# Differences of sequence blocks in a spectral layer: formed at their use instead of stored

## The chip, the cores and the metric

The kernel runs on one core of a Trainium2 chip. The metric is the device time of one execution in microseconds (us); less is better. The engines named here are PE (matrix products), DVE (element-wise work on vectors), ACT (copies and casts), POOL (element-wise work too, idle in the stages of this text) and SP, whose queue issues the DMA transfers.

## The reference

Four residual layers work on x, a sequence of S = 2048 rows of D = 640 numbers in float32: attention, spectral, attention, spectral. The attention layers (sliding, dilated, 32 heads) aren't touched by the change. The spectral layer, on the layer-normed x, is

```
a = x @ hid_re.T        # hidden DFT, real part
b = x @ hid_im.T        # hidden DFT, imaginary part
y = seq_re @ a - seq_im @ b
x = x + y
```

with the 2048 x 2048 DFT matrices seq_re, seq_im and the 640 x 640 matrices hid_re, hid_im as inputs. The result must agree with float32 arithmetic.

## The kernel before

The layers are li = 0 to 3; spectral ones are li = 1 and li = 3 (class LayerB). Each first multiplies the sequence matrices with x, writes the products z to DRAM, and then applies the hidden matrices in the stage called hidden here (`hid_mm`, L1393, with its operands prepared on ACT and DVE at L1365 to L1384).

Products are float32 in effect: an operand is split into a high half (ACT's cast, L1137) and a low half (DVE's subtraction, L1138), and a block product is three matmul passes over the halves. A split writes one of a ring of split buffers: 8 in li = 1, 10 in li = 3 (`views`).

The sequence product of six of the eight tiles of 256 columns is done by `pair(p)` for p = 0, 1, 2. One pair multiplies two such tiles t1, t2 by a block scheme with seven products instead of eight, in two sweeps of 8 steps each:

- The first sweep loads the blocks b11, b21, b22, b12 per step (128 x 512 numbers, 256 KB each) straight from the DFT matrix in DRAM (`s_raw`, L1126, DRAM name cs_in), splits all four, and runs 30 matmuls per step (L1148). In li = 1 it also forms t1 = b12 - b11 and t3 = b22 - b12 on DVE (L1225) and stores both in a DRAM tile tb (L1227). In li = 3 it doesn't.
- The second sweep needs x1 = b12 - b11, x3 = b22 - b12, x2 = b22 - x1 and x4 = b21 - x2. It loads x1 and x3 back from tb (L1221) and b22 and b21 from the DFT matrix, forms x2 and x4 on DVE (L1225), splits all four and runs 24 matmuls per step, in the order x2 (banks aux), x3 (t), x4 (m), x1 (xt and pq). Both spectral layers have the same DFT matrix, so li = 3 reads what li = 1 has stored.

A loaded block goes to one of nine raw buffers: five with the tag win, two xa and two slices of one tile e. A difference is formed in place, in the buffer of one of its operands. A raw buffer is free for the next load when the low half of its block has been split off; the load then goes out on SP's queue.

After the second sweep the banks are drained by ACT (L1301) and DVE (L1303 to L1313). In the last pair (p = 2) of a layer the hidden stage's operands are loaded meanwhile, and DVE starts preparing them (L1366, L1378, L1379, L1382) among the last steps. In li = 1 the first sweeps also carry the preparation of the hidden matrices (`b_prep`, L1177 to L1191).

The program is built ahead of the run: a scheduler with a cost model sets the order of the instructions on each engine, and picks among the free buffers of a tag. Inside `pair` only PE's order is written by hand (`manual_schedule`); in the hidden stage PE's and SP's are. DVE, ACT and the queue then run their lists in that order, each instruction waiting for what it needs.

## Time and profile before

| | us |
|---|---|
| median of 3 runs (1698.45 to 1706.01) | 1699.35 |
| span of the profiled execution | 1700.9 |
| its own time beside the span | not shown |
| PE busy | 1679.7 (99%) |
| DVE busy | 1339.2 (79%) |
| ACT busy | 794.0 (47%) |
| pairs of li = 1 | 438 to 735 |
| pairs of li = 3 | 1275 to 1574 |

How to read the rows below: a row of the timeline has the start, the duration, the engine, the line of the kernel, the operation, the tile written and the tiles read, their shape, a count, and in brackets the idle time before it with what released it. Tile names are those of the buffers: aux, t, m, xt and pq are banks of PE's output; win, xa and e are raw buffers; zo, e, stg, ot and pr are split buffers (e names both kinds); cs_in is the DFT matrix. A row of the stretches has begin and end, then the length, and for PE, PEld (weight load), DVE, ACT and POOL the busy time with the count, then PE's granted clock (1.00 is full), the DMA share and GB/s. A row of DMA issues ends with the size and the median from issue to landing.

### The profile page before, as it was taken

What the parts mean: (1) busy time and instruction counts of PE and PEld (TensorE: products, weight loads), DVE (VectorE), ACT (ScalarE), POOL (GpSimd) and SP (SyncE); (2) the same over time, 40 slices, a digit from 0 to 9 for tenths busy, and PEclk for the clock granted to TensorE, in tenths of its full rate; (3) what the DMA queues carried; (4) which work ended last, traced back from release to release, by engine and by line L of the source; (5) the groups of instructions that cost most, each with busy time, mean ns of one, the idle gap of its engine ahead of it and who ended that gap; (6) DMA issues with size and microseconds to landing.
All of it is one profiled execution on the core that took longest, in us unless ns stands there. A gap on an engine that the chain in (4) does not pass through costs nothing.

```text
span 1700.9 us, 25512 instructions
## 1 busy us (share of the span) xinstructions
PE 1679.7 (99%) x8558; PEld 1464.6 (86%) x8558; DVE 1339.2 (79%) x2034; ACT 794.0 (47%) x1617; POOL 625.8 (37%) x588
## 2 busy tenths in 40 slices
PE   9999999989999999999999999999999999999999
PEld 7888988868888887899988889988888888888999
DVE  6999999978588786788639999999784656657784
ACT  5664644544354443536554335444444544444231
POOL 4899999950000000000028988999400000000000
PEclk9999999999999999999999999999999999999999
DMA  8996668857899989986377866788666776787942
GB/s 295 315 322 227 221 227 307 271 206 265 287 370 322 370 270 354 351 331 225 122 226 239 270 217 204 246 284 295 212 234 208 225 228 215 242 282 270 362 164 93
DMA packets 263139, 441.13 MB, mean 259 GB/s; under 512 B 21824, under 2 KB 126016, under 8 KB 260704
## 3 DMA queue, kind: packets, MB, share of 16 engines
q1 hardware_dynamic: 259808, 437.55, 75.7%
q10 hardware_dynamic: 3200, 1.97, 0.4%
q8 instruction: 67, 1.10, 0.3%
q14 instruction: 64, 0.52, 0.1%
HBM read 319.75 MB, written 119.67 MB: 258 GB/s over the span
## 4 chain that ended last, share of the span: by engine, by line
PE 76%; DVE 10%; POOL 6%; DMA 4%; issue 2%; ACT 0%; SPq 0%; DVEq 0%; POOLq 0%; ACTq 0%
PE m L381 19%; PE t L1148 7%; PE aux L1148 7%; PE m L1148 7%; PE pq L1148 5%; PE xt L1148 5%; PE m L1393 4%; PE aux L1393 4%; PE m L1004 3%; PE t L1004 3%; DVE pr L450 2%; PE aux L531 2%; DVE pr L490 2%; POOL pr L509 2%; PE xt L1393 2%
## 5 line engine op out<-in xcount | busy, mean ns | idle before, releaser
L381 PE MATMUL m<-r,s 128*128 128x480 f32 x1920 | 434.5, 381 | 0.6 <-ACT stg L388 0.4
L381 PEld LDWEIGHTS m<-r,s 128*128 128x128 f32 x1920 | 355.4, 188 | 53.5 <-ACT stg L388 0.8
L193 POOL TENSOR_TENSOR stats<-stats,mhalf 128x1 f32<-128x1 f32 (+1 forms) x40 | 29.2, 730 | 512.2 <-ACT stats L189 503.8
L509 POOL TENSOR_TENSOR pr<-pr 128x640 f32<-128x640 f32 x126 | 207.8, 1650 | 23.1 <-DVE pr L490 21.7
L450 DVE TENSOR_TENSOR pr<-pq,win 128x1280 f32<-128x1280 f32 x128 | 189.9, 1484 | 13.8 <-DMA win<-kvb 7.8
L490 DVE TENSOR_TENSOR pr<-pq,win 128x1280 f32<-128x1280 f32 x128 | 190.3, 1487 | 3.7 <-POOL zo L511 1.2
L453 POOL TENSOR_TENSOR pr<-pr 128x640 f32<-128x640 f32 x115 | 164.9, 1434 | 11.2 <-DVE pr L450 11.2
L460 DVE TENSOR_REDUCE lg<-pr 128x64 f32<-128x640 f32 (+1 forms) x128 | 112.7, 881 | 8.0 <-POOL pr L453 7.9
L510 POOL TENSOR_TENSOR pr<-pr 128x320 f32<-128x320 f32 x126 | 112.0, 889 | 9.9
L388 ACT COPY stg<-m 128x480 f32<-128x480 f32 x128 | 71.0, 555 | 92.9 <-PE m L381 69.1
L1004 PE MATMUL m<-s,r 128*128 128x512 f32 x366 | 111.2, 392 | 1.6 <-DMA s<-c0b 1.3
L1004 PE MATMUL t<-s,r 128*128 128x512 f32 x366 | 110.3, 390 | 0.0
L531 PE MATMUL aux<-r2a,ot 128*128 128x320 f32 x540 | 84.7, 310 | 0.7 <-ACT s L369 0.7
L531 PEld LDWEIGHTS aux<-r2a,ot 128*128 128x128 f32 x540 | 81.1, 188 | 2.8 <-ACT s L369 1.2
L1004 PEld LDWEIGHTS m<-s,r 128*128 128x128 f32 x366 | 67.6, 188 | 16.1 <-DMA s<-c0b 1.9
L1004 PEld LDWEIGHTS t<-s,r 128*128 128x128 f32 x366 | 68.7, 188 | 14.5
L1137 ACT CAST zo<-win 128x512 fp32r<-128x512 f32 x76 | 47.2, 621 | 65.4 <-PE xt L1148 30.0
L423 ACT COPY pq<-qs 128x320 f32<-128x320 f32 x64 | 27.5, 430 | 106.0 <-DVE pr L490 73.4
L1138 DVE TENSOR_TENSOR zo<-win,zo 128x512 fp32r<-128x512 f32 x76 | 52.1, 688 | 23.7 <-ACT zo L1137 23.3
L511 POOL TENSOR_TENSOR zo<-pr 128x160 f32<-128x160 f32 x126 | 67.1, 532 | 9.9
L1004 PE MATMUL xt<-s,r 128*128 128x512 f32 x183 | 68.6, 389 | 0.0
L468 ACT ACTIVATE lg<-lg 128x128 f32<-128x128 f32 x64 | 20.3, 317 | 74.6 <-DVE lg L479 74.4
(531 smaller groups left out, 3650.2 us busy)
## 6 DMA issues: line engine op xcount, KB each, us to landing
win<-cs_in SPq DMA_DIRECT2D x192, 256.0 KB, 3.8
win<-kvb SPq DMA_DIRECT2D x96, 440.0 KB, 5.3
win<-kvb SPq DMA_DIRECT2D x64, 360.0 KB, 5.0
kvb<-stg SPq DMA_DIRECT2D x60, 320.0 KB, 4.9
xa<-cs_in SPq DMA_DIRECT2D x66, 256.0 KB, 3.6
e<-cs_in SPq DMA_DIRECT2D x64, 256.0 KB, 3.9
r<-zb SPq DMA_DIRECT2D x12, 1280.0 KB, 5.9
win<-tb SPq DMA_DIRECT2D x56, 256.0 KB, 4.4
```

The lines of the kernel that those rows point to most:

```text
L381: nc.tensor.matmul(mt[g][:, : 3 * F], st[:, a, k], wq[q][:, b, k], start=n == 0, stop=n == 14)
L388: nc.scalar.copy(sgs[q][:, :, j % 2], mt.pop(g)[:, : 3 * F].rearrange("p (a f) -> p a f", f=FE))
L450: nc.vector.tensor_tensor(pr, q, wview(u, jp, 0, [[1, FE]]), op=ALU.mult)
L453: nc.gpsimd.tensor_tensor(pv[:, :, 0:10], pv[:, :, 0:10], pv[:, :, 10:20], op=ALU.add)
L460: nc.vector.tensor_reduce(lgs[u][:, :, 2 * jp : 2 * jp + 2].rearrange("p h j w -> p (j w) h"), prq.pop((u, jp)), axis=AX.X, op=ALU.add,)
L490: nc.vector.tensor_tensor(pr.rearrange("p j w (h d) -> p j w h d", d=DH), lgs[u][:, :, 2 * jp : 2 * jp + 2].rearrange("p h j w -> p j w h" ...
L509: g.tensor_tensor(pr[:, :, 0:4], pr[:, :, 0:4], pr[:, :, 4:8], op=ALU.add)
L510: g.tensor_tensor(pr[:, :, 0:2], pr[:, :, 0:2], pr[:, :, 2:4], op=ALU.add)
L531: nc.tensor.matmul(m[:, :320], oT[(c, j)][:, a, k], wo_s["w"][:, b, k, e * 320 : (e + 1) * 320], start=(i, k) == (0, 0), stop=(i, k) == (2 ...
L1004: self.last = nc.tensor.matmul(self.z[t][k], self.xn[c][:, a, j, k * P : (k + 1) * P], self.ct[s][:, b], start=s == 0 and i == 0, stop=s = ...
L1148: nc.tensor.matmul(bank, w(a, kb), hl[b], start=start and (a, b) == (0, 0), stop=stop and (a, b) == (1, 0), skip_group_check=True,)
L1393: nc.tensor.matmul(bank[:, :320], s[:, a, k], w[:, b], start=start and (k, a, b) == (0, 0, 0), stop=stop and (k, a, b) == (KD - 1, 1, 0), ...
```

## The change

The DRAM tile tb goes, with its stores in li = 1 and its reloads in both layers. First sweeps form no differences. Second sweeps load b11, b12, b22 and b21 from the DFT matrix and form x1, x3, x2, x4 from them on DVE, in that order in the code. Products and results stay as they were.

```diff
--- before.py
+++ after.py
@@ -130,7 +130,6 @@
     qb = [[dr.tile([P, 2, NJ, FE], F32, name=f"qb_{c}_{q}") for q in range(NQ)] for c in range(NC)]
     xcb = [{m: dr.tile([P, NP, 2, 256], F32, name=f"xc_{l}_{m}") for m in (1, 2, 4)} for l in range(2)]
     zb = [[dr.tile([P, 4, KD, P], F32, name=f"zb_{l}_{t}") for t in range(NT)] for l in range(2)]
-    tb = [dr.tile([P, NP, 2, 512], F32, name=f"tb_{p}") for p in range(NPAIR)]
     wbd = dr.tile([P, NB * KD, 2, 320], F32, name="wbd")
     c0b = dr.tile([P, NST, 2, 512], F32, name="c0b")
     wob = dr.tile([P, 2, KD, D], F32, name="wob")
@@ -1205,26 +1204,14 @@
             views = [("zo0", 1), ("zo1", 1), ("e0", 1), ("stg", 2), ("zo2", 1), ("e1", 1), ("stg", 2), ("ot", 1)]
             if self.li == 3:
                 views += [("pr2", 1), ("pr3", 1)]
-            names = ("t1", "t3")
-
             def raw(t, s):
                 return self.s_raw(t, s, tags)
 
             def split(x):
                 return self.s_split(x, views)
 
-            def t_slot(n, i):
-                return tb[p][:, i, names.index(n)].rearrange("p (r t) -> p r t", r=2)
-
-            def t_raw(n, i):
-                x = self.s_buf(tags)
-                nc.sync.dma_start(x, t_slot(n, i))
-                return x
-
-            def t_sum(n, i, o, a, b):
+            def t_sum(o, a, b):
                 v.tensor_tensor(o, a, b, op=ALU.subtract)
-                if n in names:
-                    nc.sync.dma_start(t_slot(n, i), o)
                 return o
 
             def k1(i):
@@ -1264,9 +1251,6 @@
                     self.product(f2, self.x_plain(*k2(i), 512), p22, i == 0, False)
                     p12 = split(b12)
                     self.product(f2, self.x_plain(*k1(i), 512), p12, False, i == NP - 1)
-                    if sums:
-                        t_sum("t1", i, b11, b12, b11)
-                        t_sum("t3", i, b12, b22, b12)
                     self.flush()
                     if self.bprep and (p == 0 or i > 1):
                         next(self.bprep, None)
@@ -1286,12 +1270,14 @@
                 self.nx = 0
                 for i in range(NP):
                     ends = i == 0, i == NP - 1
-                    x1, b22, x3, b21 = t_raw("t1", i), raw(t2, NP + i), t_raw("t3", i), raw(t1, NP + i)
+                    b11, b12, b22, b21 = raw(t1, i), raw(t2, i), raw(t2, NP + i), raw(t1, NP + i)
+                    x1 = t_sum(b11, b12, b11)
                     s1, s2, s3 = (self.x_slot(m, i, XTAGS) if last and (m, i) in self.xlate else self.x_kept(m, i) for m in (1, 2, 3))
-                    x2 = t_sum("t2", i, b22, b22, x1)
+                    x3 = t_sum(b12, b22, b12)
+                    x2 = t_sum(b22, b22, x1)
                     self.product(q, s2, split(x2), False, i == NP - 1)
                     self.product(r, s3, split(x3), *ends)
-                    x4 = t_sum("t4", i, b21, b21, x2)
+                    x4 = t_sum(b21, b21, x2)
                     self.product(w, self.x_plain(*k2(i), 256), split(x4), *ends)
                     self.product(y, s1, split(x1), *ends)
                     self.flush()
```

Which instructions stand where on the engines, before and after, follows from the scheduler. Line numbers are smaller by 1 to 14 in the new kernel: the difference is L1225 before and L1214 after, the low half L1138 and L1137, the hidden product L1393 and L1379. The number behind a tile's name is that of the buffer's use.

The first place is DVE in the middle of a first sweep of li = 1 (its first pair). Before, one step with the two differences, and with a preparation of the hidden matrices behind them:

```order
L1138 TENSOR_TENSOR zo_756_4790<-win_4781,zo_756_4790 128x512
L1138 TENSOR_TENSOR stg_4749<-win_4726,stg_4749 128x512
L1138 TENSOR_TENSOR zo_757_4799<-win_4783,zo_757_4799 128x512
L1225 TENSOR_TENSOR win_4781<-win_4787,win_4781 128x512
L1138 TENSOR_TENSOR e_758_4808<-xa_4785,e_758_4808 128x512
L1138 TENSOR_TENSOR stg_4826<-win_4787,stg_4826 128x512
L1225 TENSOR_TENSOR win_4787<-xa_4785,win_4787 128x512
L147 SCALAR_TENSOR_TENSOR pr_751_4778<-pr_741_4716,pr_751_4778 128x2x320
```

After, at the same place:

```order
L1137 TENSOR_TENSOR zo_756_4779<-win_4770,zo_756_4779 128x512
L1137 TENSOR_TENSOR stg_4742<-win_4719,stg_4742 128x512
L1137 TENSOR_TENSOR zo_757_4788<-win_4772,zo_757_4788 128x512
L1137 TENSOR_TENSOR e_758_4797<-xa_4774,e_758_4797 128x512
L1137 TENSOR_TENSOR stg_4815<-win_4776,stg_4815 128x512
L146 SCALAR_TENSOR_TENSOR pr_751_4767<-pr_741_4709,pr_751_4767 128x2x320
```

The two L1225 rows are gone, and each raw buffer is free at its split.

The second place is DVE in li = 1's last second sweep. Before, the rows of one step: both differences, x2 and x4, then the four splits:

```order
L1225 TENSOR_TENSOR win_7110<-win_7110,xa_7108 128x512
L1225 TENSOR_TENSOR win_7113<-win_7113,win_7110 128x512
L1138 TENSOR_TENSOR zo_1142_7119<-win_7110,zo_1142_7119 128x512
L1138 TENSOR_TENSOR stg_7138<-win_7113,stg_7138 128x512
L1138 TENSOR_TENSOR e_1143_7128<-e_724_4650,e_1143_7128 128x512
L1138 TENSOR_TENSOR ot_7147<-xa_7108,ot_7147 128x512
```

After, eight rows from the same stretch; the differences of step 3 (x1 into xa_7047, x3 into win_7049, x2 into e_724, and the first of step 4, into xa_7097) stand between the splits of step 2:

```order
L1214 TENSOR_TENSOR xa_7047<-win_7049,xa_7047 128x512
L1137 TENSOR_TENSOR zo_1134_7009<-win_6998,zo_1134_7009 128x512
L1137 TENSOR_TENSOR zo_1135_7018<-e_724_4647,zo_1135_7018 128x512
L1214 TENSOR_TENSOR win_7049<-e_724_4647,win_7049 128x512
L1137 TENSOR_TENSOR e_1136_7028<-win_7000,e_1136_7028 128x512
L1214 TENSOR_TENSOR e_724_4647<-e_724_4647,xa_7047 128x512
L1137 TENSOR_TENSOR stg_7037<-win_6995,stg_7037 128x512
L1214 TENSOR_TENSOR xa_7097<-win_7099,xa_7097 128x512
```

A step has eight rows in place of six, and the first of them reads two loads into buffers that splits two steps earlier have freed.

The third place is PE at the end of li = 3's last second sweep. Before, the last step's products are complete before the hidden stage's first burst (L1393):

```order
L1148 MATMUL m_2363_15055<-zo_2433_15439,r_1_1904_12264 128x512 x3
L1148 MATMUL m_2364_15056<-zo_2433_15439,r_1_1904_12264 128x512 x3
L1148 MATMUL xt_15057<-zo_2434_15448,zo_2421_15363 128x512 x3
L1148 MATMUL pq_15058<-zo_2434_15448,zo_2421_15363 128x512 x3
L1393 MATMUL aux_2449_15507<-r2a_15109,r_2_2409_15307 128x320 x15
```

After:

```order
L1147 MATMUL m_2363_15036<-zo_2433_15436,r_1_1904_12213 128x512
L1379 MATMUL aux_2449_15504<-r2a_15092,r_2_2409_15298 128x320 x15
L1147 MATMUL m_2363_15036<-zo_2433_15436,r_1_1904_12213 128x512 x2
L1147 MATMUL m_2364_15037<-zo_2433_15436,r_1_1904_12213 128x512 x3
L1147 MATMUL xt_15038<-zo_2434_15445,zo_2421_15357 128x512 x3
L1147 MATMUL pq_15039<-zo_2434_15445,zo_2421_15357 128x512 x3
L1379 MATMUL aux_2450_15505<-r2a_15092,r_2_2409_15298 128x320 x15
```

One burst of the hidden stage, into the first aux bank, now stands ahead of the last eleven matmuls of the sweep. On SP's queue the 48 stores are gone and 96 reloads have become loads of cs_in; POOL's rows are the same.

## The prediction

> **What bounds the kernel now.** I read the page's busy shares first, then a table of stretches (one per sweep, cut where PE's step pattern changes), then PE's waits inside the spectral layers.
>
> ```profile
> span 1700.9 us, 25512 instructions
> PE 1679.7 (99%) x8558; PEld 1464.6 (86%) x8558; DVE 1339.2 (79%) x2034; ACT 794.0 (47%) x1617; POOL 625.8 (37%) x588
> 635.20:691.48 56.28, 54.95 (x241) 44.97 (x240) 35.13 (x56) 21.06 (x35) 0.00 (x0) 1.00 0.99 353
> 691.48:735.00 43.52, 43.52 (x193) 36.04 (x192) 37.92 (x58) 23.98 (x39) 0.00 (x0) 1.00 0.83 294
> ...
> 1525.70:1574.00 48.30, 48.30 (x214) 39.98 (x213) 36.63 (x56) 24.67 (x42) 0.00 (x0) 1.00 0.78 270
> PE t L1148 <- ACT zo L1137: 1.1, 1, 1.1
> PE t L1148 <- DVE zo L1138: 0.2, 1, 0.2
> PE pq L1148 <- DVE s L1311: 0.2, 1, 0.2
> PE xt L1148 <- DVE s L1311: 0.2, 1, 0.2
> ```
>
> PE is busy 1679.7 of 1700.9 us, so at most 21 us can be won in the whole program. The three stretches are li=1's last first sweep, li=1's last second sweep and li=3's last second sweep with a little of what stands ahead of it. Behind the stretch's length come busy time and count of PE, PEld, DVE, ACT and POOL, then granted clock, DMA share and GB/s. In the second sweeps PE is busy for the whole stretch at clock 1.00. The four wait rows are all that PE waited in li=1's three pairs (430 to 740 us); the same question for li=3's pairs (1275 to 1575 us) answers with no row. So the edited code runs at PE's pace, and a gain is limited to those waits.
>
> PE's pace and DVE's are two stretches of the timeline:
>
> ```profile
> 696.92 1.52 PE L1148 MATMUL aux<-zo,s 128*128 128x512 f32 x6
> 698.28 1.52 PE L1148 MATMUL t<-e,r 128*128 128x512 f32 x6
> ...
> 702.36 1.52 PE L1148 MATMUL aux<-zo,zo 128*128 128x512 f32 x6
> 697.04 0.68 DVE L1138 TENSOR_TENSOR zo<-e,zo 128x512 fp32r<-128x512 f32 x1
> 697.64 0.68 DVE L1138 TENSOR_TENSOR e<-win,e 128x512 fp32r<-128x512 f32 x1
> 698.25 0.68 DVE L1138 TENSOR_TENSOR stg<-win,stg 128x512 fp32r<-128x512 f32 x1
> 698.85 0.68 DVE L1225 TENSOR_TENSOR win<-win,xa 128x512 f32<-128x512 f32 x1
> ```
>
> A product's six matmuls take 698.28 − 696.92 = 1.36 us, and a second-sweep step, aux to aux, 702.36 − 696.92 = 5.44. DVE's 512-wide subtraction, whether split (L1138) or difference (L1225), starts 0.60 us behind the one before it: (698.85 − 697.04) / 3 = 0.603, although 0.68 is recorded.
>
> **The stores that go.** One store tile is written in li=1 only:
>
> ```profile
> L1227 SPq DMA_DIRECT2D tb<-win x27: 319/327/1104, 425.9 to 681.1; - x27
> DMA to landing us min/median/max: 2.0/4.6/6.2
> L1126 SPq DMA_DIRECT2D win<-cs_in x158: 327/333/1402, 420.3 to 1554.8; - x158
> DMA to landing us min/median/max: 2.5/3.9/7.6
> ```
>
> There are 3 pairs × 8 steps × 2 = 48 stores (27 from win buffers) of 256 KB, 4.2 MB in each li=1 first sweep, where the DMA share is 0.99. SP issues 48 fewer at 0.33 us. What can be won is what PE waits there: 1.1 + 0.2 on the splits, and at most 0.2 + 0.2 more on bank evacuations that DVE does. I take −1.3, bounds 0 and −1.7. The 96 reloads become 96 loads of the DFT matrix, of the same size and on the same queue. All transfers on the stored tile land in a median 4.6 us and all plain loads in 3.9. The count per step stays four, so I put this swap at 0.
>
> **DVE's differences.** In li=1 48 subtractions move from the first sweeps to the second ones (a first sweep loses 16 × 0.60 = 9.6 us of DVE work); in li=3 48 are new. A second-sweep step goes from six to eight of these ops, 8 × 0.603 = 4.82 us against PE's 5.44. By throughput they are hidden, with 0.62 a step to spare. In the last pair of each layer, hidden-DFT preparation shares DVE, and that cover is gone for two or three steps; there the lead that DVE has built up must carry it.
>
> **The new way that loads come round.** This is the term on which the forecast rests. A step needs four of nine raw buffers. Before, the first split of a step needed two loads (the stored difference and b22); now x2 = b22 − (b12 − b11) needs three, and the third is issued one split later. From the release of a buffer by a split to the difference that reads its refill, three round trips in li=3's middle pair and one in li=1's last show the size:
>
> ```profile
> 708.98 0.69 DVE L1138 TENSOR_TENSOR stg<-xa,stg 128x512 fp32r<-128x512 f32 x1 [0.85 <-ACT stg L1137]
> 709.70 0.33 SPq L1126 DMA_DIRECT2D xa<-cs_in  x1
> 714.46 0.69 DVE L1225 TENSOR_TENSOR xa<-xa,win 128x512 f32<-128x512 f32 x1 [1.03 <-DMA xa<-cs_in]
> 1437.56 0.69 DVE L1138 TENSOR_TENSOR ot<-xa,ot 128x512 fp32r<-128x512 f32 x1
> 1438.53 0.38 SPq L1126 DMA_DIRECT2D xa<-cs_in  x1
> 1442.75 0.69 DVE L1225 TENSOR_TENSOR xa<-xa,win 128x512 f32<-128x512 f32 x1 [1.80 <-DMA xa<-cs_in]
> 1445.77 0.68 DVE L1138 TENSOR_TENSOR stg<-win,stg 128x512 fp32r<-128x512 f32 x1
> 1446.48 0.33 SPq L1126 DMA_DIRECT2D win<-cs_in  x1
> 1449.55 0.69 DVE L1225 TENSOR_TENSOR win<-win,e 128x512 f32<-128x512 f32 x1 [0.94 <-DMA win<-cs_in]
> 1450.76 0.68 DVE L1138 TENSOR_TENSOR ot<-xa,ot 128x512 fp32r<-128x512 f32 x1
> 1451.47 0.33 SPq L1126 DMA_DIRECT2D xa<-cs_in  x1
> 1455.79 0.69 DVE L1225 TENSOR_TENSOR xa<-xa,win 128x512 f32<-128x512 f32 x1 [0.97 <-DMA xa<-cs_in]
> ```
>
> From the split's end to the difference's start: 714.46 − 709.67 = 4.8, 1442.75 − 1438.25 = 4.5, 1449.55 − 1446.45 = 3.1, 1455.79 − 1451.44 = 4.35. I call this d; the mean is 4.2. The lead that absorbs it is how far DVE's splits run ahead of PE, limited by the split buffers (8 in li=1, 10 in li=3):
>
> ```profile
> 625.21 0.69 DVE L1138 TENSOR_TENSOR ot<-e,ot 128x512 fp32r<-128x512 f32 x1 [0.67 <-ACT ot L1137]
> 633.84 0.84 PE L1148 MATMUL xt<-ot,r2a 128*128 128x512 f32 x3
> 1464.74 0.69 DVE L1138 TENSOR_TENSOR pr<-win,pr 128x512 fp32r<-128x512 f32 x1 [0.67 <-ACT pr L1137]
> 1476.08 1.30 PE L1148 MATMUL aux<-pr,r 128*128 128x512 f32 x5
> 720.02 0.82 DVE L1378 TENSOR_TENSOR e<-r 128x640 f32<-128x640 f32 x1
> ...
> 721.49 0.68 DVE L1138 TENSOR_TENSOR stg<-win,stg 128x512 fp32r<-128x512 f32 x1
> ```
>
> Split end to matmul is 633.84 − 625.90 = 7.9 us in li=1 and 1476.08 − 1465.43 = 10.65 in li=3. A 640-wide preparation op costs (721.49 − 720.02) / 2 = 0.735.
>
> Now the dependences, counted along DVE's new order (each buffer followed by name from the split that frees it to the difference that reads its next load). In li=1's last pair, from the split of x1 in step 0 to the split of x4 in step 7, the longest chain holds 36 ops of 512, 8 of 640 and five round trips: 36 × 0.603 + 8 × 0.735 + 5d = 27.6 + 5d. PE needs between those two products 6.75 steps, 36.7 us. PE stands still for 27.6 + 5d − 36.7 − 7.9 = 5d − 17.0: at d = 3.1 nothing, at 4.0 3.0, at 5.0 8.0. In li=3's last pair the chain holds 39 and 12 ops and four trips: 32.3 + 4d − 36.7 − 10.65 = 4d − 15.0, so 0, 1.0 and 5.0. The other four second sweeps stay inside their leads: the nearest to its limit, li=1's first, has 29 ops, one preparation of 640 and five trips, 18.2 + 5d against seven steps' 38.1 and the lead of 7.9, and stalls from d = 5.6 only.
>
> I take d = 4.0, a little under the mean, because only trips that DVE had to wait for could be read off; those that came in time are not among them. That gives 3.0 + 1.0 = +4.0. The ends are the least and the largest quoted, 3.1 (nothing) and 4.8 (7.0 + 4.2).
>
> [...]
>
> **PE's own order** is altered at one place, the end of li=3's last second sweep: the first hidden burst (15 matmuls into aux) now stands ahead of the last eleven matmuls of step 7. It needs the copy of the aux bank by ACT (L1301) 11 × 0.227 = 2.5 us sooner than before. If it must wait for that copy, the bounds are 0 and 1.1, the largest wait for ACT in the rows above. I take 0.2, because seven matmuls (1.6 us) still lie between aux's last product and the burst.
>
> **Sum.** −1.3 + 0 + 4.0 + 0.2 = +2.9 on the profiled execution's 1700.9 us. Its own time beside the span isn't shown; the span is 1.5 us above the median of 1699.35 us, so I add the difference to the median: 1702.2, said as 1702 us.
>
> **The rivals.**
> *Loads come round too slowly (slower).* With more traffic d is longer. The two last pairs also fetch the hidden layer's operands:
>
> ```profile
> win<-cs_in SPq DMA_DIRECT2D x6, 256.0 KB, 5.4
> win<-cs_in SPq DMA_DIRECT2D x13, 256.0 KB, 2.9
> ```
>
> The first row is li=1's last second sweep, where loads into this tile land in a median 5.4 us; the second is li=3's middle one, with 2.9. If all trips in both last pairs carry 1 us more (d = 5.0), the waits are 8.0 + 5.0 and the result +11.9, about 1711; with the full 2.5 us more that the rows differ by (d = 6.5) it is 15.5 + 11.0, about 1725. This becomes slower by over 0.5% from a stall of 9.8 us, where 9d − 32.0 = 9.8: d = 4.6. For it: the one trip quoted from that pair is the longest. Against it: that pair's trip had a landing inside its 4.8, so 5.4 is not the landing of every load, and before the change PE waits nowhere in these stretches.
>
> *DVE itself becomes the bound (slower).* If each op held DVE for the recorded 0.69, a step would need 5.52 against 5.44, and the chains would grow by 36 × 0.09 = 3.2 and 3.5 us; with d = 4.0 the stall is 6.2 + 4.5, the result +9.6, about 1709. The quoted starts 0.60 apart speak against it. [...]
>
> *Relief of the DMA queue (faster).* In li=1's first sweeps 4.2 MB of about 20 per sweep go (353 GB/s × 56.28 us). But PE waits only 1.7 there, so alone this gives 1697.6, not a measurable gain.
>
> *The cover holds (no change).* PE hides every difference and load: with the stores' relief 1698, without it 1699.
>
> **How the numbers follow.** This measurement can tell about 0.5%, 8.5 us, from no change: below 1690.9 and above 1707.8. My forecast (d between 3.1 and 4.6, with small stalls) has 0.45, and no stall with or without the 1.3 us gain 0.23: together 0.68 within 0.5%. Slow loads have 0.24, DVE's longer ops 0.03, the moved burst or something else in the new order that costs over 8 us 0.02: 0.29 slower. Faster has 0.03, since no row shows 8.5 us to win. The range runs from 1696 (all bounds on the good side, 1699.35 − 1.7, and the spread of the three runs shown) to 1714 (d = 5.2, 9.0 + 5.8 of stall); beyond it I leave the worse half of the slow loads.
>
> **What would show it.** PE's waits in li=1's first sweeps should be near zero, and DMA share there fall by a fifth. In the second sweeps DVE's busy time should rise to 8 ops a step. New waits of PE should name ACT or DVE splits of the spectral line and lie only in steps 3 to 7 of the last pairs, a few us together. Behind the end of li=3's last sweep aux should not wait. I am wrong if PE waits in first or middle pairs too, if DVE's starts spread past 0.60 without a wait, or if the time falls below 1691 us.

## The result, and the profile after

The changed kernel takes 1717.91 us (median of 4 runs, 1716.14 to 1718.88); the kernel before, run beside it, takes 1702.49 (4 runs, 1698.45 to 1706.01). The ratio is 1.009, with a 95% interval of 1.0068 to 1.0111: slower by 15 us. The forecast of no change was wrong, and the time lies above the range (1696 to 1714). The side was that of the first rival. Its cause was another one, as the experiments show.

The page of the changed kernel, its first rows:

```profile
span 1714.0 us, 25517 instructions
PE 1686.6 (98%) x8558; PEld 1467.3 (86%) x8558; DVE 1361.3 (79%) x2082; ACT 789.6 (46%) x1617; POOL 626.0 (37%) x588
```

The span has grown by 13.1 us. PE runs the same 8558 matmuls, and DVE has 48 instructions more. The waits of PE in li = 1's pairs (430 to 740 us) and then in li = 3's (1275 to 1600 us); the columns are total, number and longest:

```profile
PE aux L1147 <- ACT zo L1136: 2.5, 1, 2.5
PE aux L1147 <- DVE zo L1137: 2.4, 3, 1.3
PE aux L1147 <- ACT s L1259: 1.1, 1, 1.1
PE xt L1147 <- DVE s L1297: 0.9, 1, 0.9
PE m L1147 <- DVE s L1292: 0.6, 2, 0.4
PE pq L1147 <- DVE s L1297: 0.2, 1, 0.2
...
PE aux L1147 <- DVE pr L1137: 1.2, 1, 1.2
PE aux L1147 <- DMA zo<-xc: 0.2, 1, 0.2
```

Before there were 1.7 us of such waits in li = 1 and none in li = 3; now there are 7.7 and 1.4. They name splits (L1136 on ACT, L1137 on DVE), copies and sums of finished banks (L1259, L1292, L1297) and, in li = 3, one load. The table of stretches of the changed kernel, for the last pair's two sweeps (cut about 1 us ahead of the start of each):

```profile
639.00:692.80 53.80, 53.80 (x239) 44.55 (x239) 32.09 (x49) 21.08 (x35) 0.00 (x0) 1.00 0.87 294
692.80:745.00 52.20, 48.45 (x202) 39.34 (x201) 43.63 (x68) 23.54 (x41) 0.00 (x0) 0.93 0.74 256
```

The relief of the DMA queue is there: the last first sweep moves 294 GB/s where it moved 353. The last second sweep has become the worst stretch, with a wait of PE and a granted clock of 0.93 where it was 1.00.

To see where the time went, I compare the start of the second product (bank t) of each sweep in the two traces. In the first pair's second sweep, for instance, it starts at 494.22 before and 494.89 after, so PE is 0.7 us behind there. The table holds this lag, in us, against the profiled execution of the kernel before (positive is behind), for the experiments too (their names are those used below). "End of li=1" is the end of the last pair's last product; the last column is the difference of the spans:

| kernel | li=1 starts | last pair starts | its second sweep | end of li=1 | li=3's last second sweep | span |
|---|---|---|---|---|---|---|
| the change | −0.7 | 4.8 | 2.9 | 9.7 | 10.6 | 13.1 |
| before, again | −0.4 | −0.3 | −1.4 | −1.4 | −0.6 | −0.8 |
| only li=3 changed | −1.5 | 0.1 | −1.0 | −1.0 | −1.2 | 1.0 |
| only li=1's second sweeps | −2.4 | 0.6 | 6.3 | 13.0 | 11.4 | 11.5 |
| differences later | 0.4 | 9.7 | 7.8 | 13.1 | 13.1 | 20.3 |
| x1, x3 on POOL | −0.5 | 14.4 | 13.6 | 22.0 | 25.1 | 31.4 |
| no x1, x3 | −1.3 | 4.4 | 2.5 | 2.5 | 2.7 | 7.0 |
| before, two more ops | −0.1 | 0.9 | −0.6 | 0.3 | 0.3 | 5.4 |
| preparation of hidden operands later | −1.2 | 4.8 | 2.9 | 4.0 | 5.2 | 5.4 |
| preparation of hidden matrices later | 1.5 | 0.6 | −1.3 | 2.4 | 1.9 | 4.6 |
| both preparations later | 1.0 | 2.4 | 0.5 | 0.5 | 2.3 | 2.3 |
| all three later | −0.4 | 0.9 | −1.0 | −0.2 | −0.2 | −0.1 |

The 13.1 us of the change are thus: −0.7 ahead of the pairs, +5.5 in the first two pairs of li = 1, −1.9 in its last first sweep, +6.8 in its last second sweep, +0.9 between the layers, and +2.5 from li = 3's last second sweep on. Two executions of one kernel differ by up to 1.4 us in a column ("before, again"), so differences of that size carry nothing.

The largest piece is a single stall. The timeline of the changed kernel at the last step of li = 1, first PE, then DVE, then ACT:

```profile
735.08 0.80 PE L1147 MATMUL aux<-zo,pr 128*128 128x512 f32 x1 [2.48 <-ACT zo L1136]
737.16 2.50 PE L1147 MATMUL aux<-zo,pr 128*128 128x512 f32 x5 [1.28 <-DVE zo L1137]
739.45 2.68 PE L1147 MATMUL t<-e,r 128*128 128x512 f32 x6
741.97 1.55 PE L1147 MATMUL m<-stg,r 128*128 128x512 f32 x6
...
731.08 1.55 DVE L1352 TENSOR_TENSOR r<-r,r 128x640 fp32r<-128x640 f32 x2
...
733.27 0.69 DVE L1214 TENSOR_TENSOR xa<-xa,win 128x512 f32<-128x512 f32 x1
...
735.68 0.82 DVE L1352 TENSOR_TENSOR zo<-r,zo 128x640 fp32r<-128x640 f32 x1
736.42 0.69 DVE L1137 TENSOR_TENSOR zo<-xa,zo 128x512 fp32r<-128x512 f32 x1
...
733.79 0.72 ACT L1351 CAST zo<-r 128x640 fp32r<-128x640 f32 x1
734.42 0.61 ACT L1136 CAST zo<-xa 128x512 fp32r<-128x512 f32 x1
```

x2 of step 7 is formed at 733.27 into xa, cast at 734.42 and has its low half at 736.42. Ahead of it stand two preparation ops of 640 on DVE (L1352 at 731.08), one more ahead of its low half (735.68), and a preparation cast on ACT (L1351) ahead of its cast. PE, which needs x2 first of the four, waits 2.48 + 1.28 = 3.76 us. It loses more: from the first aux matmul to the second are 2.08 us in place of 0.23, the five behind it take 739.45 − 737.16 = 2.29 in place of 1.13, the six of t take 2.52 in place of 1.36. With the 2.48 that is 1.85 + 1.16 + 1.16 more, 6.7 us, the whole lag of that sweep. Its granted clock (third number from the end) in the 10 us around the wait and in the piece in which it is low:

```profile
730.00:740.00 10.00, 6.25 (x20) 4.42 (x19) 9.88 (x15) 5.15 (x9) 0.00 (x0) 0.75 0.34 135
735.07:741.90 6.83, 5.54 (x12) 4.11 (x13) 5.69 (x10) 3.63 (x6) 0.00 (x0) 0.50 0.16 33
```

So some 2.9 of the 6.7 us are a lower clock behind the wait, and 3.8 are the wait.

The second place is the first pair's second sweep, ACT, PE and DVE of the changed kernel:

```profile
492.14 0.74 ACT L144 ACTIVATE pr<-pr 128x640 fp32r<-128x640 f32 x1 [3.85 <-DMA wbd<-pr]
492.78 1.05 ACT L1259 COPY s<-aux 128x512 f32<-128x512 f32 x2
493.40 1.66 PE L1147 MATMUL aux<-zo,r2a 128*128 128x512 f32 x6 [1.10 <-ACT s L1259]
499.75 1.42 PE L1147 MATMUL aux<-zo,r2a 128*128 128x512 f32 x5 [0.39 <-DVE zo L1137]
...
497.68 0.69 DVE L1214 TENSOR_TENSOR win<-xa,win 128x512 f32<-128x512 f32 x1 [2.74 <-DMA xa<-cs_in]
499.01 0.69 DVE L1137 TENSOR_TENSOR zo<-win,zo 128x512 fp32r<-128x512 f32 x1
```

An op of the hidden matrices' preparation (`b_prep`, L144) holds ACT for 3.85 us, because the tile it writes is still being stored (wbd). The copy of bank aux stands behind it, and PE behind the copy. In step 1 DVE waits 2.74 us for a load, and the split of x2 (499.01) comes as late.

### The profile page after: what moved, and what is told of

It reads as the page before. It is cut to its first block, busy times and chain, and to the rows that moved or that the text cites. A ratio compares the mean times of both kernels' runs of the same rounds, so it can differ in the third digit from the quotient of the medians.

```text
span 1714.0 us, 25517 instructions
## 1 busy us (share of the span) xinstructions
PE 1686.6 (98%) x8558; PEld 1467.3 (86%) x8558; DVE 1361.3 (79%) x2082; ACT 789.6 (46%) x1617; POOL 626.0 (37%) x588
## 4 chain that ended last, share of the span: by engine, by line
PE 54%; DVE 19%; DMA 13%; POOL 8%; issue 4%; ACT 2%; SPq 1%; DVEq 0%; ACTq 0%; POOLq 0%
PE m L380 11%; PE aux L1147 5%; PE t L1147 5%; PE m L1147 5%; DVE pr L449 4%; PE aux L1379 4%; PE pq L1147 4%; PE xt L1147 4%; DVE pr L489 3%; PE m L1379 3%; POOL pr L508 3%; PE m L1003 2%; PE t L1003 2%; DMA e<-cs_in 2%; POOL pr L452 2%
## 5 line engine op out<-in xcount | busy, mean ns | idle before, releaser
L1136 ACT CAST zo<-win 128x512 fp32r<-128x512 f32 x76 | 47.1, 621 | 75.7 <-PE xt L1147 38.9
L1137 DVE TENSOR_TENSOR zo<-win,zo 128x512 fp32r<-128x512 f32 x76 | 52.0, 688 | 20.2 <-ACT zo L1136 19.9
L1147 PE MATMUL t<-e,r 128*128 128x512 f32 x204 | 53.0, 396 | 0.0
```

What stands on the lines that cost most here:

```text
L1147: nc.tensor.matmul(bank, w(a, kb), hl[b], start=start and (a, b) == (0, 0), stop=stop and (a, b) == (1, 0), skip_group_check=True,)
```

## The experiments

Each is compared with the kernel before, run on the same chip; ratios have 95% intervals. The first question was which layer loses.

**One layer at a time.** The store tile stays in both kernels; the named layer alone loads plain blocks.

```diff
+                    plain = self.li == 3      # the other kernel: == 1
+                    if plain:
+                        x1, x3, b22, b21 = raw(t1, i), raw(t2, i), raw(t2, NP + i), raw(t1, NP + i)
+                        v.tensor_tensor(x1, x3, x1, op=ALU.subtract)
+                    else:
+                        x1, b22, x3, b21 = t_raw("t1", i), raw(t2, NP + i), t_raw("t3", i), raw(t1, NP + i)
...
+                    if plain:
+                        v.tensor_tensor(x3, b22, x3, op=ALU.subtract)
```

> Only li=3 is changed: li=1 still stores its two differences and reloads them, li=3 loads plain blocks and forms all four differences on VectorE. Three theories. (H) DVE takes its list in order, so a difference that waits for a load holds up splits that are ready behind it, and the lead over PE is used up; what tips it over in li=1 is the work that rides along there (b_prep in the first pairs, hidden preparation in the last). (D) DVE has too many instructions where other work rides along. (L) it is the load's round trip alone, in whatever layer. From the trace of the changed kernel PE lost 10.4 us over li=1's pairs and 2.0 over li=3's. H and D expect about +2 us on the kernel before (+1.5 of waits in li=3's last pair, nothing in li=1). L, by which both last pairs should lose alike, expects half of the whole loss, +6 to +7.

> Only li=1's second sweeps are changed: they load plain blocks and form four differences; li=1's first sweeps still form and store the two differences, and li=3 still reads them. H and D expect the loss of li=1 to be here in full: the changed kernel's +10.4 over li=1, and about 1.9 more because the wait in li=1's last first sweep (which the removed stores ended) stays: +11 to +14 on the kernel before. L expects +6. If the first sweeps' differences and stores cost nothing, the sum of this run's and the first run's differences is the whole change's 13 to 15; if their removal helped, the sum is larger by 2.

Only li = 3: 1706.73 us, 1.0023 (1.0009 to 1.0037). Only li = 1's second sweeps: 1714.59, 1.0067 (1.005 to 1.0083). Both are nearer to what (H) and (D) expected than to (L). The shares add up to the whole (0.23% + 0.67% = 0.90%), but in part by luck, since in the second kernel the loss lies elsewhere than in the change. 6.7 us of it are in the last pair's second sweep (2.4 of them a hidden burst that PE now runs ahead of the sweep's end; behind it the lag is 10.6), and 5.7 in the first sweep ahead of it, which in this kernel still forms and stores the differences. These 5.7 are one wait:

```profile
PE t L1148 <- ACT zo L1137: 5.2, 1, 5.2
```

The cast that PE waits for stands on ACT behind one that waits 2.95 us for a load (until 668.61). So this run doesn't tell what the stores that go are worth.

li = 3, with two more split buffers and no hidden matrices to prepare, loses little, and only in its last second sweep.

**The order on DVE.** In the changed kernel the scheduler puts the differences of the next step between the splits of this one. Here those of a step are issued behind all four low halves of the step before.

```diff
-                    x1 = t_sum(b11, b12, b11)
...
-                    x3 = t_sum(b12, b22, b12)
-                    x2 = t_sum(b22, b22, x1)
+                    with ExitStack() as es:
+                        for lo in self.los[-4:]:      # the last four low halves
+                            es.enter_context(tc.issue_after(lo))
+                        x1 = t_sum(b11, b12, b11)
+                        x3 = t_sum(b12, b22, b12)
+                        x2 = t_sum(b22, b22, x1)
+                        x4 = t_sum(b21, b21, x2)
...
-                    x4 = t_sum(b21, b21, x2)
```

> The changed kernel with one rule on VectorE's order: the four differences of a step stand behind the four splits of the step before. Nothing else is changed: same loads, same instructions, same buffers. H expects the leads at the start of li=1's first pair's second sweep to come back to 4 us or more and most of the loss to go: +0 to +5 on the kernel before. D (number of instructions) and L (round trip) both expect no change: +13 to +16.

It is slower still: 1723.7 us, 1.0122 (1.0106 to 1.0139), which none of the three theories expected. But in li = 1's last second sweep the lead came back. The low half of x1 of step 5 in li = 1's last second sweep, and the matmul that reads it (tile ot), in the kernel before, in the change, and with the order changed:

```profile
715.07 0.68 DVE L1138 TENSOR_TENSOR ot<-win,ot 128x512 fp32r<-128x512 f32 x1
722.76 0.84 PE L1148 MATMUL xt<-ot,xr 128*128 128x512 f32 x3
```
```profile
722.98 0.69 DVE L1137 TENSOR_TENSOR ot<-win,ot 128x512 fp32r<-128x512 f32 x1
725.64 0.84 PE L1147 MATMUL xt<-ot,xr 128*128 128x512 f32 x3
```
```profile
721.97 0.69 DVE L1138 TENSOR_TENSOR ot<-win,ot 128x512 fp32r<-128x512 f32 x1
730.59 0.84 PE L1148 MATMUL xt<-ot,xr 128*128 128x512 f32 x3
```

From the split's end to its use: 722.76 − 715.75 = 7.0 us before, 725.64 − 723.67 = 2.0 after, 730.59 − 722.66 = 7.9 with the order changed. What DVE waited for in that sweep, in the change (all waits for loads) and with the order changed (the two longest; no row names a load):

```profile
DVE win L1214 <- DMA e<-cs_in: 4.5, 2, 3.7
DVE win L1214 <- DMA xa<-cs_in: 2.8, 2, 2.2
DVE xa L1214 <- DMA win<-cs_in: 1.4, 1, 1.4
```
```profile
DVE r L1356 <- ACT r L1355: 1.9, 1, 1.9
DVE s L1293 <- PE t L1148: 1.7, 1, 1.7
...
```

8.7 us of waits for loads are gone, with the same loads and the same subtractions. In the change DVE was waiting for a load while splits whose block had landed stood behind the waiting difference: the difference at 715.34 waits 2.15 us, and behind it stand the low halves of 715.95 and 717.15, whose casts ACT had done by 712.7. Still PE stalls again at step 7 (1.0 + 2.1 us), in li = 3 for 0.9 + 3.6 us, and most is lost in the first pair: within its second sweep the lag grows from 1.9 to 10.2 us. DVE waits for no load there either (488 to 548 us); what it waits for longest is the preparation of the hidden matrices, whose ops L144 and L148 are:

```profile
DVE pr L148 <- ACT pr L144: 3.3, 2, 1.7
```

So the short lead is not enough as a reason: other work stands ahead of the late split.

**x1 and x3 on POOL**, which is idle there (0.00 us in the stretches above).

```diff
-            def t_sum(o, a, b):
-                v.tensor_tensor(o, a, b, op=ALU.subtract)
+            def t_sum(o, a, b, on=v):
+                on.tensor_tensor(o, a, b, op=ALU.subtract)
...
-                    x1 = t_sum(b11, b12, b11)
+                    x1 = t_sum(b11, b12, b11, nc.gpsimd)
...
-                    x3 = t_sum(b12, b22, b12)
+                    x3 = t_sum(b12, b22, b12, nc.gpsimd)
```

> The changed kernel with x1 and x3 formed on GpSimd, which is idle in the pairs, so VectorE has six instructions a step again, as before. A 512-wide subtraction there is estimated at 1.3 us from the 640-wide one of 1.65 us, 2.6 a step against 5.44. D expects the loss to go: -1 to +3 on the kernel before. H expects most of it to go as well, since only x2 and x4 wait on VectorE now, but x2 waits for GpSimd: +2 to +8. L expects it to stay and grow by the slower subtraction: +13 to +18.

The slowest of all: 1733.63 us, 1.0174 (1.0159 to 1.0189), beyond every expectation. The timeline of this kernel, POOL and DVE in the first pair's second sweep:

```profile
504.37 1.39 POOL L1214 TENSOR_TENSOR win<-xa,win 128x512 f32<-128x512 f32 x1
509.26 1.53 POOL L1214 TENSOR_TENSOR e<-win,e 128x512 f32<-128x512 f32 x1 [3.50 <-DMA win<-cs_in]
...
504.57 1.75 DVE L1137 TENSOR_TENSOR zo<-win,zo 128x512 fp32r<-128x512 f32 x1
506.24 0.68 DVE L1137 TENSOR_TENSOR e<-e,e 128x512 fp32r<-128x512 f32 x1
509.55 1.79 DVE L1137 TENSOR_TENSOR e<-win,e 128x512 fp32r<-128x512 f32 x1
```

The two DVE ops that meet one of POOL in these rows take 1.75 and 1.79 us in place of 0.68, 1.1 more, where the move was to save DVE 0.60 an op. So this run says nothing of what DVE's load costs; it has a price of its own.

**No x1 and x3 at all.** The blocks as loaded take their place (so x1 and x3 are not the differences): the loads, the buffers and x2's three operands stay, DVE has six ops a step.

```diff
-                    x1 = t_sum(b11, b12, b11)
+                    x1, x3 = b11, b12
...
-                    x3 = t_sum(b12, b22, b12)
```

> The changed kernel without the two added subtractions: x1 and x3 are taken as the plain blocks b11 and b12, so x2 = b22 - b11 and x4 = b21 - x2, and the results of the pairs are no longer the reference's. Loads, their source, the missing stores and all else are the changed kernel's; VectorE has six instructions a step in the second sweeps again, as in the kernel before. (D) the added instructions on VectorE are the cause: the loss goes, -3 to +1 us on the kernel before. (L) the loads from the DFT matrix in place of the stored tile, or their round trip through the buffers, are the cause: most of the loss stays, +8 to +14.

1712.55 us, 1.0054 (1.0037 to 1.007), as (L) expected. In li = 1's last second sweep the loss of 6.8 us is gone. The one up to the last pair remains (from −1.3 to 4.4), so it doesn't come from the added subtractions.

**The kernel before with two more DVE ops a step**, max(x, x) on the reloaded x1 and x3:

```diff
+                    for x in (x1, x3):
+                        v.tensor_tensor(x, x, x, op=ALU.max)
```

> The kernel before with two more VectorE instructions in every step of the second sweeps: the loaded x1 and x3 are replaced in place by the maximum of themselves and themselves, which changes no value. Loads and stores are those of before, the first sweeps of li=1 still form and store the differences. (D) expects the changed kernel's loss, and more in li=1, whose first sweeps keep their 16 subtractions: +11 to +18 us. (L) expects -1 to +3.

1709.27 us, 1.0036 (1.0023 to 1.0049), between the two expectations. In li = 1, where the change loses 10.4 us, eight ops a step cost 0.4. The loss that there is comes at the end of li = 3, where the load of a hidden operand is late. Its row in this kernel (the one without x1 and x3 has the like, with 2.2 us):

```profile
PE aux L1148 <- DMA zo<-xc: 2.9, 1, 2.9
```

Neither the ops alone nor the plain loads alone give the loss in the last second sweep; together they do.

**The riding work.** Two kinds of work share ACT and DVE with the pairs: the hidden operands' preparation in the last pair, and the hidden matrices' (`b_prep`) in li = 1's first sweeps. Two rules on the changed kernel, one by one and together: the first puts the hidden operands' preparation behind the four splits of the last step; the second puts an instalment of `b_prep` behind the first split of its own step.

```diff
 # first rule; preparations 0 and 1 are now called behind the step loop
+            with ExitStack() as es:
+                for lo in self.los[-4:]:
+                    es.enter_context(tc.issue_after(lo))
+                self.prep_now(step)
 # second rule
-                        next(self.bprep, None)
+                        with tc.issue_after(self.los[-4]):
+                            next(self.bprep, None)
```

> The changed kernel with one rule on VectorE's order: the hidden stage's preparation may not stand ahead of the last four splits of the layer's last pair. The number of instructions is the same. If the 6.8 us at the end of li=1's last second sweep and the 1.5 to 2 at the end of li=3's come from the preparation standing ahead of the split that PE needs first (O), they go or shrink to the 2.2 us by which VectorE's work there exceeds PE's (45.7 against 43.5), and the result is +5 to +9 on the kernel before, with the granted clock back at 1.00. If the lead is used up by the loads' round trips and VectorE's count alone (D or L), the stall stays: +12 to +16.

> As the run before, and b_prep, the preparation of the hidden matrices that rides in li=1's pairs, may not stand ahead of the first split of the first-sweep step that it belongs to. In the changed kernel ten or so of its instructions have run ahead into the first pair's second sweep. (D) VectorE has 44.5 us of recorded work in that sweep's 49.0 us, so with some 5 us of it moved to the next first sweep, the 5.5 us lost there go or shrink to 1 to 2: 0 to +4 us on the kernel before for the whole. (L) expects that loss to stay: as the run before.

> The changed kernel with the rule on b_prep alone: it may not stand ahead of the first split of its own first-sweep step; the hidden preparation stands where it stood in the changed kernel. If the order of the riding work is the cause in both places and the two places are independent (O), the 5.5 us between the start of li=1's first second sweep and its second pair shrink to 1 to 2, as with both rules, and the 6.8 at the end of li=1's last pair and some 2 in li=3 stay: +8 to +11 us on the kernel before. If the lead that b_prep's place costs in the first pair is what the last pair lacks, that goes too: 0 to +3.

First rule: 1707.36 us, 1.0024 (1.0014 to 1.0033). Second: 1707.51, 1.0025 (1.0012 to 1.0038). Both: 1703.41, 1.0001 (0.9991 to 1.0012). Each takes away the part that it aims at. With the first, li = 3's pairs have no wait, and the last second sweep of li = 1 loses 1.1 us in place of 6.8 (another 1.0 goes behind it, where the first hidden burst waits for the copy of aux); up to the last pair it still loses 6.0. With the second that part is gone (from 1.5 to 0.6), and all waits that PE still has in the pairs lie at the two ends, li = 1's (first two rows) and li = 3's:

```profile
PE aux L1148 <- ACT zo L1137: 1.8, 1, 1.8
PE aux L1148 <- DVE zo L1138: 1.4, 1, 1.4
...
PE aux L1148 <- DVE pr L1138: 1.7, 1, 1.7
```

The second rule does more than it aims at: the last second sweep of li = 1 loses 3.7 us in place of 6.8, and behind its waits the six matmuls of t take 734.74 − 733.38 = 1.36 us, no longer than in the kernel before. So the two places are not independent, as the expectation of +8 to +11 us had them.

With both, nothing measurable of the change's 15 us is left, although all plain loads and all four differences on DVE are there. Where the second rule acts can be read from the starts of bank t. In the change, 1.4 us are lost at step 0 of the first pair's second sweep and 0.7 at step 1 (the stalls quoted above), 1.5 at steps 6 and 7, and 1.9 at the first step of the second pair. At step 6 PE waits 0.72 us for the split of x2 (528.01); the longest wait of the last place, in the changed kernel:

```profile
545.59 1.63 PE L1147 MATMUL xt<-zo,r 128*128 128x512 f32 x6 [0.93 <-DVE s L1297]
```

With the second rule alone PE doesn't wait at all from 486 to 553 us. The stall quoted at 493.40 has its like with both rules, with ACT held for 3.83 us, but only 0.2 us of it reach PE. The riding work itself isn't new: ten of `b_prep`'s ops start on DVE in this sweep in the kernel before, as in the change (none with the rule). But before, ACT copies bank aux at 487.56, as soon as it is finished, and in the change the copy stands behind the op that is held.

**The same rules in the kernel before**, with a second run of that kernel as it is:

> The kernel before once more, for a second trace of it: which of its small waits come back? The 1.1 + 0.2 us in li=1's last first sweep, on which the forecast's gain of 1.3 rests, are absent from the changed kernel, but also from two kernels that keep the stores. If the removed stores ended them, they are here again. If they vary from execution to execution, they are absent or have another size. The time is that of before within 0.3%.

> Both rules (b_prep not ahead of its own step's first split, hidden preparation not ahead of the last pair's last four splits) in the kernel before. (O) the rules mend what the changed order broke, and the kernel before has leads of 5 us and more where they act: -2 to +2 us. If the rules were a gain of their own, unconnected with the change, the kernel before would gain as the changed one did: -10 to -14, which PE's total wait of 2 us in these pairs excludes.

As it is: 1702.15 us, 0.9998 (0.9988 to 1.0009). With both rules: 1714.04, 1.0065 (1.005 to 1.008). Up to the start of li = 1's last second sweep the rules gain at most a little: PE goes from 0.2 us behind to 2.5 ahead, and the second run of the kernel as it is from 0.4 to 1.4 ahead. So they are no gain of their own that would hide a loss of the size of the change's. Their own loss there, which the expectation didn't have, is one wait, at the start of that sweep:

```profile
PE xt L1149 <- ACT pr L1285: 11.1, 1, 11.1
```

A copy of a finished bank goes into a tile that the postponed `b_prep` still holds: a mishap of this kernel's order, not a sign of the lead.

**Is it the third load that x2 needs?** The prediction's new dependence was that x2 needs three loads and not two. Two kernels without x1 and x3 as differences, with two ops of max(x, x) in their place, were to give x2 two operands at eight ops a step.

```diff
-                    x1 = t_sum(b11, b12, b11)
+                    x1, x3 = b11, b12
+                    for x in (x1, x3):
+                        v.tensor_tensor(x, x, x, op=ALU.max)
...
-                    x3 = t_sum(b12, b22, b12)
 # the second kernel also issues its loads in the order b11, b22, b12, b21
```

> As the run without the two added subtractions (x1 and x3 are the plain blocks, so the pairs' results are not the reference's), but with two instructions in their place that replace x1 and x3 by the maximum of themselves and themselves. So VectorE has eight instructions a step as in the changed kernel, but x2 needs two loads, as before, not three. Read from it is VectorE's lead in steps 2 to 6 of li=1's last second sweep: 2 to 4 us in the changed kernel, 5 to 7 without the two instructions. (D) the instructions use it up: 2 to 4 here. (L) the third load does: 5 to 7 here. Time: +4 to +12 us on the kernel before, since b_prep's place stays open.

> As the run of the plain blocks with two maxima in place of the two added subtractions (results of the pairs not the reference's), but the loads are issued in the order b11, b22, b12, b21 instead of b11, b12, b22, b21. In the earlier run x2 = b22 - b11 named two loads, but the second of them was issued third, so it did not test what its expectation said. Here the first split really needs the first two loads only, as in the kernel before. (L3) the third-issued load is what VectorE waits for: its waits for DMA in li=1's second sweeps fall from 4 to 8 us each to at most 3, its lead in the last one rises from 0 or 1 to 4 and more, and the time falls from +25 to +3 to +8 us. (S) the plain source is slower than the stored tile, whatever the order: waits, leads and time stay, +20 to +27.

1728.32 us, 1.0148 (1.0127 to 1.0169), and 1725.13, 1.013 (1.0114 to 1.0146). The first doesn't test what its expectation says, since b22 is still the third load issued. The second does: x2 needs two loads, the first two, and the kernel is slower than the change. DVE waits 13.6 us for loads ahead of the ops of li = 1's last second sweep, against 10.2 in the change (8.7 of them are in the rows above). So the loss doesn't go when x2 no longer needs the third load. The time is that of (S), but (S) can't be right: with both rules the same plain loads cost nothing. Compared with the kernel without the max ops (1712.55), the last second sweep loses 6.7 us and not 0: there, eight ops and plain loads lose only together. Why the max ops cost more than the subtractions that they stand for I can't say.

**PE's order of products**: x1, whose operands land first, ahead of x2 in steps 1 to 7; and the same with both rules.

```diff
+                    if i:
+                        self.product(y, s1, split(x1), *ends)
...
-                    self.product(q, s2, split(x2), False, i == NP - 1)
+                    if not i:
+                        self.product(q, s2, split(x2), False, False)
                     self.product(r, s3, split(x3), *ends)
+                    if i:
+                        self.product(q, s2, split(x2), False, i == NP - 1)
...
-                    self.product(y, s1, split(x1), *ends)
+                    if not i:
+                        self.product(y, s1, split(x1), *ends)
```

> The changed kernel with another order of the four products of a second-sweep step (all but the first step): x1 = b12 - b11 first, which needs the first two loads, then x3, which needs the third, then x2 and x4. Same loads, same instructions, same results. (L3) the wait for the third load at a step's head is half of the cause: leads in li=1's second sweeps rise by the 1.36 us of a product or more, most stalls go, +1 to +7 us on the kernel before. (O alone) the place of the riding work is the whole cause: no change, +13 to +17.

> The run before with both rules on VectorE's order (b_prep not ahead of its own step's first split, the hidden preparation not ahead of the last pair's last four splits). If both causes hold, no stall is left in the pairs beside evacuations of banks: -2 to +1 us on the kernel before. A gain of more than 3 us is excluded, since PE waits less than 2 us in the kernel before's pairs.

1713.52 us, 1.0063 (1.0048 to 1.0078), between the two expectations, and with the rules 1708.67, 1.0042 (1.0026 to 1.0059), slower than expected. The late split is no longer the first that PE needs, but aux is finished later, and the first hidden burst waits for its copy at the end of each layer, 2.0 us in li = 1 and here 3.0 in li = 3 (with the rules 0.5 and 3.9):

```profile
PE aux L1385 <- ACT s L1293: 3.0, 1, 3.0
```

**All three orders at once**: the differences behind the splits, and both rules.

> The changed kernel with all three rules on VectorE's order: the differences of a step stand behind the four splits of the step before (the third run), b_prep not ahead of its own step's first split, the hidden preparation not ahead of the last pair's last four splits (the eighth). In the third run the lead in li=1's last second sweep held at 4.6 to 7.9 us through steps 2 to 5, where the changed kernel has 2 to 4, although instructions and loads are the same; its loss lay in li=1's first pair and in the last two steps of both last pairs, where the riding work stands. (H+O) the order of the differences uses up the lead, and the riding work's place turns it into a stall: with both mended, leads of 4 us and more to step 7 in both last pairs, no stall, -2 to +2 us on the kernel before. (O alone) +0.3, as the eighth run, with leads of 1 to 3 again in the middle pairs. (L, D: loads or count) stalls of 5 us or more stay in the last pairs.

1702.88 us, 0.9996 (0.9985 to 1.0007). Beside the change the order of the differences cost some 6 us (1723.7 − 1717.9); with the rules it costs nothing. All that PE waits in li = 1's pairs (in li = 3's it doesn't wait):

```profile
PE aux L1148 <- ACT s L1261: 1.1, 1, 1.1
PE aux L1148 <- DVE zo L1138: 0.5, 1, 0.5
PE pq L1148 <- ACT zo L1269: 0.2, 1, 0.2
```

The time is what (H+O) expected; the leads of 4 us and more are not there. In li = 1's last second sweep the low half of x2 of step 6 ends at 723.90, and PE waits 0.5 us for it (the second row); that of step 7 ends at 729.22, 0.1 us ahead of its use. DVE waits 3.1 us for loads in that sweep. So a thin lead costs nothing here as long as nothing else stands ahead of the split that PE needs.

This and the kernel with both rules do what the change set out to do, with 428.5 MB of transfers in place of 441.1, and are as fast as the kernel before. None is faster: PE's work sets the time, as the prediction's first part read it (PE is busy 1679.7 of 1700.9 us before, and with all three orders it waits 1.8 us in the pairs).

## Why the prediction was wrong

**The bound** was read rightly: PE's pace, and no gain to be had beyond a few waits. So was DVE's pace: its ops stay 0.60 apart (in the change, low halves start at 711.29, 711.89 and 712.49), eight a step fit, and in li = 1 eight a step cost the kernel before 0.4 us.

**The stores.** The DMA rate fell by about a sixth in the last first sweep (353 to 294 GB/s), the DMA share from 0.99 to 0.87. The −1.3 can't be shown: that sweep gains 1.9 us in the change, but a second execution of the kernel before gains 1.1 in it as well. The wait on which the term rested differs from one execution to the next (1.1 + 0.2 us in the profile before, 0.2 in the second one), and one profile can't tell that.

**The loads, +4.0.** This is the step that failed. Its sizes for the last pairs, 3.0 and 1.0 us, lie near the waits of PE that came (3.8 and 1.2), but that is luck, since another chain made them. Three things in it were wrong.

1. "The other four second sweeps stay inside their leads." They were granted the lead of 7.9 us seen elsewhere before. In the first pair's second sweep x2 of step 0 had 2.3 us when PE used it (its split ends at 491.1, the matmul starts at 493.40), and x2 of step 1 came late. The first two pairs lost 5.5 us where the sum had 0; with the second rule alone they lose none. `b_prep`, which stands on ACT and DVE at that very place, was taken as one preparation op of 0.735 us; that ACT can be held for 3.85 us by a store ahead of such an op was left out of the sum.
2. "From the split of x1 in step 0 to the split of x4 in step 7." The chain was followed to the last split in DVE's order. PE needs x2 first, and x2 of step 7 stands behind the preparation of hidden operands on both engines that make it. The stall sat there, 3.8 us of waits, in a chain that ends earlier and whose slack is smaller: in the kernel before, the low half of x2 of step 7 ends at 726.18 and is used at 729.56, a lead of 3.4 us and not 7.9.
3. A wait was priced at its length. Behind the 3.76 us the granted clock fell, and 6.7 were lost. PE's longest wait in the kernel before, 2.1 us at 352.6, leaves the granted clock at 1.00, so that profile couldn't show it. In the change the six matmuls of t took 2.52 us in place of 1.36 while the granted clock was 0.50 (735.07 to 741.90), and the first matmul behind the wait of 2.48 us already took 0.80 in place of 0.39.

**The rival "loads come round too slowly"** had the sign and nearly the size, for a reason that the runs refute. It needed trips of over 4.6 us. Landing in li = 1's last second sweep became quicker, not slower. DMA issues of that sweep, before and after:

```profile
win<-cs_in SPq DMA_DIRECT2D x6, 256.0 KB, 5.4
```
```profile
win<-cs_in SPq DMA_DIRECT2D x11, 256.0 KB, 4.2
```

The trips that DVE waited for in that sweep of the change were of the size that the sum took: xa was free at 711.98 and read at 715.34, 3.4 us; e was free at 698.15 and read at 702.55, 4.4 us. What was new is that DVE waited for them (8.7 us, before 1.0), and with the same loads it waits for none in that sweep once the differences stand behind the ready splits.

**"DVE itself becomes the bound"** is refuted by the op count in the kernel before, **"the cover holds"** by the result, though it is what both rules make true.

**The moved burst**, +0.2: nothing to be seen. The last matmuls and bursts of li = 3 (1584 to 1591 us) run without a wait.

**What would show it.** I had written that I am wrong if PE waits in first or middle pairs too. It did.

In short, the change puts a queue in order that costs nothing by the count of its work: differences that wait for loads, between splits that are ready, with riding work in front of the split that PE needs next. The first eats the lead; the second turns a lead of 1 to 4 us (x2, steps 1 to 6 of li = 1's last second sweep) into a stall. That each rule takes away its part is shown; that the lead matters on its own is not, since the order that restores it gained nothing without the rules, and with them the time is the same with and without it.

What stays open: by what the plain loads make `b_prep`'s place cost 5.6 us in the first two pairs even with six DVE ops a step, while the kernel before with eight loses 1.0 there; why the max ops are so dear; and the 1.9 us of the last first sweep.

## What to carry to other kernels

When work moves onto an in-order engine that has time to spare, counting its time isn't enough: list what stands ahead of the next instruction that the bounding engine needs, above all waits for loads and work for a later stage (here a difference that waited 2.15 us for its load held up two splits whose casts were done). Take the lead of each place from that place, and check the chain that ends in the first operand needed, not in the last one issued. If a change that should be free is slower, try moving the riding work back before giving the change up: here two such rules took away all of a 0.9% loss.

## What the runs showed of the hardware

**A wait of PE can cost more than its length.** 3.76 us cost 6.7 here, with a granted clock of 0.75 in the 10 us around it. In the kernel before with two more ops, li = 3's last second sweep has a wait of 2.94 us (until 1544.89); behind it the six matmuls of t take 1549.08 − 1546.52 = 2.56 us in place of 1.36, and the lag grows by 5.1 from there to the end. Not every wait of this length does it: in the second kernel with max ops in place of x1 and x3, PE waits 2.86 us at the same place (until 1563.86), and the six matmuls of t take 1566.75 − 1565.37 = 1.38 us. A wait of 1.10 us (493.40 above) left the six matmuls behind it at 1.66 us, against 1.52.

**The DVE ops that met one of POOL took 1.75 and 1.79 us in place of 0.68.** In the rows of the POOL kernel, POOL's ops end at 505.76 and 510.79, and the DVE ops that met them at 506.32 and 511.34: 0.56 and 0.55 later, nearly a full op. By these two rows the DVE op seems to have done its work only when POOL's was over.
